# Attention and mixture of experts on one core: softmax sums as a reduction over two columns, and batches 0 and 1 in another order

## The chip, the cores and the metric

The kernel runs on one core of a Trainium2 chip. The metric is the device time of one execution in microseconds (us), the median of several runs. The engines are called as in the profile: PE (matrix multiply, with PEld for its weight loads), DVE (vector), ACT (activation), POOL (GpSimd) and SP (which issues most DMAs). Each engine takes its instructions strictly in the order of the program.

## The reference

```python
def _attn_ref(q, k, v):                    # each (8, 8, 576, 64)
    k_p = k.reshape(B, H, Sp, pool, D).mean(axis=3)   # pool = 8, Sp = 72
    v_p = v.reshape(B, H, Sp, pool, D).mean(axis=3)
    scores = scale * np.matmul(q, k_p.transpose(0, 1, 3, 2))
    scores = scores - np.max(scores, axis=-1, keepdims=True)
    attn = np.exp(scores)
    attn = attn / (np.sum(attn, axis=-1, keepdims=True) + 1e-09)
    return np.matmul(attn, v_p)
...
def _moe_ref(x, w_group, w_expert, w1, w2):   # x (4608, 512)
    # group = argmax of x @ w_group, expert = argmax of x @ w_expert[group]: top 1 of 4, then top 1 of 4
    # out[token] = g_w * e_w * (relu(x @ w1[g, e]) @ w2[g, e]); w1 (.., 512, 1024), w2 (.., 1024, 512)
```

The rows of x are the tokens, with the 8 heads of a token side by side.

## The kernel before

The work goes batch by batch (8 batches of 576 tokens). All matrix products of x are made in two parts: a value rounded to the fast format (`hi`) and the rest (`lo`), with three products for each pair. Nearly all tokens of a batch go to one expert, so the kernel guesses that expert (batches 0 and 1) or counts it (`main_expert`, later batches), loads its weights with an address from a register, and runs all 576 tokens through it. Tokens of other experts are run in a loop at the end.

For one batch, in pieces whose names stand in the plans below (`a`, `n`, `x` are the attention of the plan's batch, the next and the one after; `m`, `w` the experts' part of the plan's batch and the next):

- `load_k`, `load_v`, `load_q`/`load_qb`: DMAs from SP. `kr`, `vr`, `vm` sum k (DVE) and v (POOL) over eight rows: the folds of L257 and L258. `kt` turns k on PE. `qb` (L303, DVE) or `qt` (PE) turns q.
- for each of five chunks `c`: `sc` (scores, PE, L317), `mx` (maximum, DVE, L328), `sb` (subtract on DVE, L333, then exp on ACT, L335), `su_` (sums and reciprocals, DVE, L341 to L343), `nm` (multiply by the reciprocal, on POOL as `:p` or DVE as `:v`, L348), `pt` (transpose, DVE, L355).
- `av` (attention times v, PE, L368, then the copies of x to `xa`/`xb` on ACT, L373), `avd` (the low part of x, DVE, L377), `rt` (router products, PE), `route_g` and `route_e` (the choice of group and expert on DVE, some 17 tiny instructions, L390 to L427), `count` (PE), `gates` (L481 to L495) and `keep_x`.
- `guess_x`, `guess_e`: the guess, from the mean of v. It ends in `elect`, whose integer (L449) SP reads into a register before the weights' DMAs (`load`, L523) go out.
- `load:m:j`: a quarter of w1 (m = 1) or w2 (m = 2), four buffers in all. `cast` makes its high part (ACT, L529), `lo` its low part (POOL, L535, in 2 or 4 pieces); `split` is both.
- `up:f:half` (12 matmuls, L552), its relu (ACT, L554) and `upd` (DVE, low part of the hidden values, L560/L564); `down:z` (8 matmuls, L578/L589) and the scaled result (L583) with its store.
- `home_v` (L205 to L210) writes the sums of v of batch 0 to memory and reads them back in another layout. `warm` is matmuls on ones, with no use but to occupy PE. `split_wr` (L859, L860) makes the router's weights in two parts.

The order within each engine is written out by hand. `START` (to the first `up`), `FIRST` (rest of batch 0) and `SECOND` (batch 1) fix it for PE, SP, DVE, ACT and POOL; `STEADY` (batches 2 to 6) and `LAST` (batch 7) fix it for all but ACT, which a planner orders by its own costs. Rings of buffers: three PSUM banks `mm` for `up`, `down`, `warm` and some `sc`; one pair of banks `sc` shared by `sc` and half of `av`; three banks `tp` for the rest.

```python
LATE = 1
MANUAL = [{ET.PE, ET.SP, ET.DVE, ET.Activation, ET.Pool}, {ET.PE, ET.SP, ET.DVE, ET.Pool}]
```

Of the kernel before, what the change touches and what calls it, by code (L numbers as in the profile page):

```python
# [919 lines left out]
```

## Time and profile before

| | us |
|---|---|
| median of 3 runs (lowest, highest) | 543.24 (542.77, 543.7) |
| the profiled execution, its own time | 541.33 |
| its span, first to last instruction | 539.7 |
| busy in the span: PE, PEld | 514.7, 450.0 |
| busy in the span: DVE, POOL, ACT | 361.2, 245.4, 208.5 |
| mean granted clock of PE | 0.99 of full speed |

Positions below are us from the start of the span. The first `up` of batch 0 starts at 28.21, that of batch 1 at 104.86, that of batch 2 at 172.39, that of batch 3 at 234.3. The profiled execution's own time is 1.6 us more than its span, and 1.9 us less than the median of the runs.

### The profile page before, as it was taken

To read this page: it belongs to the slowest core of one execution; us is meant where nothing else is said; L and a number is where in the kernel's file an instruction comes from. 1 tells how busy PE (TensorE), PEld (TensorE's weight loads), DVE (VectorE), ACT (ScalarE), POOL (GpSimd) and SP (SyncE) were. 2 spreads that over 40 slices of the span, in tenths; PEclk is the share of its full clock that TensorE was granted. 3 is DMA by queue.
4 is the path that set the end of the run, shared out by engine and by line. 5 is a ranking of instruction groups with operands and counts; after the bars stand their busy time and mean duration, and the time that the engine had idled before them with its cause. 6 is when DMAs were issued, how large, how long until landed. Compare 5 with 4: busy or idle time off the path is not lost.

```text
span 539.7 us, 15043 instructions
## 1 busy us (share of the span) xinstructions
PE 514.7 (95%) x6059; PEld 450.0 (83%) x6059; DVE 361.2 (67%) x1039; ACT 208.5 (39%) x402; POOL 245.4 (45%) x217
## 2 busy tenths in 40 slices
PE   9899798979998999999999999999999999999995
PEld 7778786879876998899888998899888988899864
DVE  6787889688767886479664966578644953287602
ACT  2264323353323652354415442355325442344211
POOL 2299426155702781276508580476409661411300
PEclk9799999999999999999999999999999999999998
DMA  8599267837155594547726592779536200835711
GB/s 281 152 237 213 28 203 190 194 104 193 36 98 186 152 247 81 195 148 213 113 76 238 168 170 57 238 281 234 93 113 209 81 3 19 267 115 202 258 72 52
DMA packets 117984, 83.75 MB, mean 155 GB/s; under 512 B 71018, under 2 KB 93546, under 8 KB 117656
## 3 DMA queue, kind: packets, MB, share of 16 engines
q1 hardware_dynamic: 113904, 75.60, 52.3%
q10 hardware_dynamic: 3976, 7.12, 3.8%
q8 instruction: 49, 0.80, 0.6%
q14 instruction: 23, 0.19, 0.1%
q0 software_dynamic: 32, 0.04, 0.0%
HBM read 77.31 MB, written 28.53 MB: 196 GB/s over the span
## 4 chain that ended last, share of the span: by engine, by line
PE 76%; DVE 11%; DMA 7%; issue 2%; ACT 2%; SPq 1%; POOL 1%; ACTq 0%; DVEq 0%; POOLq 0%
PE mm L552 31%; PE mm L578 26%; PE mm L589 5%; PE sc L317 4%; DMA sw<-in_moe_w_dram 4%; PE sc L368 4%; PE tp L385 2%; DMA vv<-in_v_dram 1%; DMA out_dram<-y 1%; DVE pT L355 1%; DVE p L333 1%; DVE mx L328 1%; DVE p L348 1%; POOL w L535 1%; DVE kv L258 1%
## 5 line engine op out<-in xcount | busy, mean ns | idle before, releaser
L535 POOL TENSOR_TENSOR w<-sw,w 128x1024 fp32r<-128x1024 f32 (+2 forms) x87 | 150.0, 1741 | 154.5 <-ACT w L529 154.5
L578 PE MATMUL mm<-w,ht 128*128 128x512 f32 x768 | 177.5, 384 | 0.0
L578 PEld LDWEIGHTS mm<-w,ht 128*128 128x128 f32 x768 | 141.4, 189 | 22.1 <-issue 2.0
L552 PE MATMUL mm<-xb,w 128*128 128x320 f32 x768 | 116.4, 303 | 3.8 <-DVE es L422 1.7
L552 PEld LDWEIGHTS mm<-xb,w 128*128 128x128 f32 x768 | 106.1, 189 | 8.1 <-issue 3.7
L552 PE MATMUL mm<-xa,w 128*128 128x256 f32 x768 | 98.1, 279 | 5.7 <-DVE ht L560 3.1
L552 PEld LDWEIGHTS mm<-xa,w 128*128 128x128 f32 x768 | 91.5, 191 | 10.5 <-DVE ht L560 3.3
L554 ACT ACTIVATE ht<-mm 128x256 fp32r<-128x256 f32 (+1 forms) x128 | 52.1, 408 | 91.5 <-PE mm L552 91.3
L529 ACT CAST w<-sw 128x1024 fp32r<-128x1024 f32 x64 | 66.1, 1043 | 26.4 <-DMA sw<-in_moe_w_dram 26.4
L348 POOL TENSOR_TENSOR p<-p,su 128x576 f32<-128x576 f32 (+1 forms) x34 | 36.6, 1079 | 55.1 <-DVE su L343 51.3
L564 DVE SCALAR_TENSOR_TENSOR ht<-mm,ht 128x160 fp32r<-128x160 f32 (+2 forms) x192 | 38.6, 257 | 14.8 <-ACT ht L554 14.3
L335 ACT ACTIVATE p<-p 128x576 f32<-128x576 f32 (+1 forms) x40 | 25.5, 638 | 58.7 <-DVE p L333 57.3
L583 ACT ACTIVATE y<-mm,gm 128x512 f32<-128x512 f32 x32 | 21.9, 684 | 48.7 <-PE mm L578 45.3
L328 DVE TENSOR_REDUCE mx<-sc 128x8 f32<-128x576 f32 (+1 forms) x38 | 26.1, 687 | 20.1 <-PE sc L317 20.1
L560 DVE SCALAR_TENSOR_TENSOR ht<-mm,ht 128x256 fp32r<-128x256 f32 x64 | 26.1, 408 | 17.6 <-ACT ht L554 17.2
L317 PE MATMUL sc<-kT,qT 64*32 64x72 f32 x2176 | 30.4, 229 | 2.6 <-DVE qT L303 1.3
L317 PEld LDWEIGHTS sc<-kT,qT 64*32 64x32 f32 x2176 | 23.8, 105 | 10.2 <-issue 6.7
L355 DVE STREAM_TRANSPOSE pT<-p 128x640 f32<-128x640 f32 (+1 forms) x40 | 30.4, 761 | 1.6 <-POOL p L348 1.5
L341 DVE TENSOR_REDUCE su<-p 128x8 f32<-128x576 f32 (+1 forms) x40 | 27.0, 674 | 4.0 <-ACT p L335 3.8
L589 PE MATMUL mm<-w,ht 128*128 128x512 f32 x128 | 29.6, 381 | 0.0
L368 PE MATMUL sc<-pT,v 32*64 32x256 f32 (+1 forms) x384 | 26.9, 409 | 1.4 <-DVE pT L355 1.4
L333 DVE TENSOR_TENSOR p<-sc,mx 128x576 f32<-128x576 f32 (+1 forms) x38 | 26.4, 694 | 1.4
(213 smaller groups left out, 529.3 us busy)
## 6 DMA issues: line engine op xcount, KB each, us to landing
sw<-in_moe_w_dram SPq DMA_DIRECT2D x72, 512.0 KB
xscr<-xb SPq DMA_DIRECT2D x8, 1280.0 KB
vv<-in_v_dram SPq DMA_DIRECT2D x27, 320.0 KB
xscr<-xa SPq DMA_DIRECT2D x8, 1024.0 KB
q<-in_q_dram SPq DMA_DIRECT2D x112, 72.0 KB
kv<-in_k_dram SPq DMA_DIRECT2D x14, 512.0 KB
out_dram<-y ACTq DMA_DIRECT2D x24, 256.0 KB
pT<-xscr SPq DMA_DIRECT2D x4, 1152.0 KB
```

The costliest lines, as they stand in the source:

```text
L317: nc.tensor.matmul(ps[x][32 * g:32 * g + 32, SP * t:SP * t + SP], lhsT=s.qT[c][64 * x:64 * x + 64, g, 32 * t:32 * t + 32], rhs=s.kT[64 * x ...
L333: tt(out=p.rearrange("p t (x s) -> p x t s", x=2)[:, x], in0=ps[:, :, 0:SP * w].rearrange("p x (t s) -> p x t s", s=SP), in1=bc(s.m[c][:, ...
L348: (nc.vector if eng == "v" else nc.gpsimd).tensor_tensor(out=p, in0=p, in1=bc(s.su[c][:, 0:w], SP), op=ALU.mult)
L355: nc.vector.transpose(out=s.pT[:, :, o:o + n].rearrange("p j (t i) -> p t j i", i=32), in_=probs[(s.b * NC + c) % 2][:, 0:n // 32].rearran ...
L368: nc.tensor.matmul(banks[a][64 * x:64 * x + 64, 0:n], lhsT=s.v6[32 * a:32 * a + 32, 5 if x and i == 0 else j, :], rhs=s.pT[32 * a:32 * a + ...
L529: nc.scalar.copy(out=s.w[m, j][0], in_=raw)
L535: (nc.vector if eng == "v" else nc.gpsimd).tensor_tensor(out=wl[:, i:i + n], in0=s.raw[m, j][:, i:i + n], in1=wh[:, i:i + n].bitcast(F32), ...
L552: nc.tensor.matmul(ps[:, 0:n], lhsT=l[:, kc, fs], rhs=apart(s.a.xt[o][:, r, kc]), start=(kc == 0 and i == 0), stop=(kc == 3 and i == 2))
L554: nc.scalar.activation(out=halves(ht[:, sl]), in_=joined(ps[:, 0:n]), func=AF.Relu)
L564: stt(out=ht[:, at:at + hi - lo], in0=ps[:, a, lo:hi], scalar=0.0, in1=ht[:, t + lo:t + hi].bitcast(F32), op0=ALU.max, op1=ALU.subtract)
L578: nc.tensor.matmul(ps, lhsT=s.ht[f][:, 640 * l + o:640 * l + o + 128], rhs=apart(s.w[2, f // 2][r][:, f % 2, :]), start=(i == 0), stop=(i ...
L589: nc.tensor.matmul(ps, lhsT=s.ht[f][:, 512:640], rhs=apart(s.w[2, f // 2][r][:, f % 2, :]), start=(i == 0), stop=(i == 15))
```

## The change

1. `su_`: two standing tiles `sums` hold 1e-9 in every second column. The sum over 72 goes to the first column, and a second reduction adds the pair; the instruction that added 1e-9 and multiplied by 8 (L342) is gone. The factor of one eighth is in the copies of x: `av` multiplies by 0.125 while it copies, `avd` is a three-operand instruction that does the same.
2. `route_e` and `gates` can put their last product on POOL (`:p`).
3. `START`, `FIRST` and `SECOND` are in another order. `STEADY` and `LAST` have the same order.

```diff
 START
-t.warm:10 t.turn_wr a.kr:0 a.kr:1 a.kt a.vr:0:f a.vr:1:f a.qt:0 a.qt:1 a.sc:0 a.mx:0 a.sb:0 a.sc:1:m a.guess_x a.mx:1 a.sb:1 a.home_v a.guess_e a.vm
-m.load:1:0 m.load:1:1 m.load:1:2 m.load:1:3 a.qt:2 a.su_:0 a.nm:0:p a.qt:3 a.su_:1 a.nm:1:p t.warm:5 n.load_v n.load_k a.sc:2:m a.qt:4 a.pt:0 a.pt:1 m.cast:1:0 m.lo:1:0:p:4
-a.av:0:256 a.mx:2 a.sb:2 m.cast:1:1 m.lo:1:1:p:4 a.avd:0:256 t.split_wr
+t.warm:10 t.turn_wr a.kr:0 a.kr:1 t.split_wr a.kt a.vr:0:f a.vr:1:f a.qt:0 a.qt:1 a.sc:0 a.mx:0 a.sc:1:m t.warm:2 a.guess_x a.sb:0 a.mx:1 a.home_v a.guess_e a.qt:2 a.sb:1 a.su_:0 a.nm:0:p
+m.load:1:0 m.load:1:1 m.load:1:2 m.load:1:3 a.qt:3 a.su_:1 a.nm:1:p a.vm a.sc:2:m a.qt:4 t.warm:7 n.load_v n.load_k a.pt:0 a.pt:1 m.cast:1:0 m.lo:1:0:p:4
+a.av:0:256 a.mx:2 a.sb:2 m.cast:1:1 m.lo:1:1:p:4 a.avd:0:256
 FIRST (its first two lines stand, but for m.up:0:0, now m.up:0:0:1)
-m.up:5:0 a.pt:4 n.vr:0 m.cast:2:0 m.lo:2:0:p:2 m.upd:5:0 m.up:6:0 m.upd:6:0 a.av:256:320 m.up:7:0 a.rt:0:256 m.upd:7:0 a.avd:256:320 n.kr:0
-n.vr:1 n.vm m.up:0:1:1 m.upd:0:1 n.kr:1 a.rt:256:320 m.cast:2:1 m.lo:2:1:p:2 m.up:1:1 m.upd:1:1 m.up:2:1 a.route_g m.upd:2:1 m.up:3:1 m.cast:2:2 m.lo:2:2:p:2 a.route_e m.upd:3:1 m.up:4:1 m.upd:4:1
-n.kt m.up:5:1 m.upd:5:1 a.count n.guess_x m.cast:2:3 m.lo:2:3:p:2 n.qb:0 m.up:6:1 n.guess_e w.load:1:0 w.load:1:1 m.upd:6:1 n.sc:0 n.mx:0 n.sb:0 n.qb:1 a.gates a.keep_x m.up:7:1 m.upd:7:1
-m.down:0 n.su_:0 n.nm:0:p w.load:1:2 m.down:1 w.load:1:3 n.sc:1 n.mx:1 n.sb:1 n.pt:0 n.qb:2 m.down:2 m.store:0 x.load_v x.load_k m.down:3 n.su_:1 n.nm:1:p w.split:1:0:p:2 m.down:4 n.sc:2 n.mx:2 n.sb:2 n.pt:1 n.qb:3
-m.down:5 m.store:1 w.split:1:1:p:2 n.su_:2 n.nm:2:v n.av:0:256 n.avd:0:256 m.down:6 n.sc:3 n.mx:3 n.sb:3 n.pt:2 n.qb:4 m.down:7 n.su_:3 n.nm:3:v n.sc:4 n.mx:4 n.sb:4 m.down:8 m.store:2 x.vr:0
-n.rt:0:256 n.pt:3 n.su_:4 n.nm:4:v w.load:2:0 w.load:2:1 x.load_qb:0 m.down:9 n.pt:4 x.kr:0 m.down:10 n.av:256:320 n.avd:256:320 x.kr:1 x.vr:1 x.vm m.down:11 m.store:3 x.load_qb:1 x.load_qb:2 x.load_qb:3 n.rt:256:320 m.down:12 n.route_g m.down:13 m.store:4
+m.up:5:0 a.pt:4 n.vr:0 m.upd:5:0 m.up:6:0 m.upd:6:0 a.av:256:320 n.vr:1 n.vm m.up:7:0 a.rt:0:256 m.upd:7:0 a.avd:256:320 n.kr:0
+m.up:0:1:1 m.upd:0:1 n.kr:1 a.rt:256:320 n.guess_x m.cast:2:0 m.up:1:1 n.guess_e m.upd:1:1 a.route_g m.cast:2:1 m.up:2:1 m.upd:2:1 a.route_e:p m.lo:2:0:p:2 m.up:3:1 m.upd:3:1 m.lo:2:1:p:2 m.cast:2:2 a.gates m.up:4:1 m.upd:4:1
+a.count n.qb:0 m.lo:2:2:p:2 n.kt m.cast:2:3 m.up:5:1 m.upd:5:1 a.keep_x n.sc:0 n.mx:0 n.sb:0 n.qb:1 m.lo:2:3:p:2 m.up:6:1 w.load:1:0 w.load:1:1 m.upd:6:1 n.su_:0 n.nm:0:p m.up:7:1 m.upd:7:1
+m.down:0 w.load:1:2 n.sc:1 n.mx:1 n.sb:1 n.pt:0 n.qb:2 m.down:1 w.load:1:3 m.down:2 m.store:0 n.su_:1 n.nm:1:p x.load_v x.load_k w.split:1:0:p:2 m.down:3 n.sc:2 n.pt:1 n.mx:2 n.sb:2 n.qb:3 n.qb:4 m.down:4 n.su_:2 n.nm:2:p n.av:0:256 n.avd:0:256 w.split:1:1:p:2
+m.down:5 m.store:1 n.sc:3 n.mx:3 n.sb:3 n.pt:2 m.down:6 n.su_:3 n.nm:3:p m.down:7 n.sc:4 n.mx:4 n.sb:4 n.pt:3 x.load_qb:0 m.down:8 m.store:2 n.su_:4 n.nm:4:p x.vr:0 n.rt:0:256 w.load:2:0 w.load:2:1 m.down:9 n.pt:4 x.kr:0 n.av:256:320 n.avd:256:320
+m.down:10 x.kr:1 x.vr:1 x.vm x.load_qb:1 x.load_qb:2 x.load_qb:3 n.rt:256:320 m.down:11 m.store:3 n.route_g m.down:12 n.route_e:p n.gates:p m.down:13 m.store:4
 SECOND (its first line before and after; further down, before: m.down:7 n.route ... m.down:9 n.main_expert; after: m.down:5 n.route_g n.route_e:p ... m.down:7 n.main_expert)
-m.up:0:0 m.upd:0:0 m.split:1:2:p:2 m.load:2:2 a.route_e m.up:1:0 m.upd:1:0 m.split:1:3:p:2 m.load:2:3 m.up:0:1 m.upd:0:1 m.split:2:0:p:2 m.up:1:1 m.upd:1:1 m.up:2:0 a.count m.upd:2:0 a.gates a.keep_x m.up:2:1
+m.up:0:0 m.upd:0:0 n.qb:0 m.up:1:0 m.upd:1:0 m.split:1:2:p:2 m.load:2:2 a.count n.kt m.up:0:1 m.upd:0:1 a.keep_x m.split:1:3:p:2 m.load:2:3 m.up:1:1 m.upd:1:1 n.sc:0 n.mx:0 n.sb:0 n.qb:1 m.up:2:0 m.upd:2:0 n.su_:0 n.nm:0:p m.split:2:0:p:2 m.up:2:1 m.upd:2:1 n.sc:1 n.mx:1 n.sb:1 n.pt:0 n.qb:2
...
+    sums = [keep.tile([128, 4, 2, 2], F32, name=f"s{i}") for i in range(2)]
+    for t in sums:
+        nc.vector.memset(t, 1e-9)
...
-            su = su[:, 0:w]
-            red(out=su, in_=p.rearrange("p t (x s) -> p t x s", x=2), axis=AX.X, op=ALU.add)
-            ts(out=su, in0=su, scalar1=1e-9, scalar2=8.0, op0=ALU.add, op1=ALU.mult)
+            su, two = su[:, 0:w], sums[(s.b * NC + c) % 2][:, 0:w]
+            red(out=two[:, :, :, 0], in_=p.rearrange("p t (x s) -> p t x s", x=2), axis=AX.X, op=ALU.add)
+            red(out=su, in_=two, axis=AX.X, op=ALU.add)
...
-                nc.scalar.copy(out=xt[:, 0, g], in_=ps)
+                nc.scalar.mul(out=xt[:, 0, g], in_=ps, mul=0.125)
...
-                tt(out=s.xt[o][:, 1, g], in0=ps, in1=s.xt[o][:, 0, g].bitcast(F32), op=ALU.subtract)
+                stt(out=s.xt[o][:, 1, g], in0=ps, scalar=0.125, in1=s.xt[o][:, 0, g].bitcast(F32), op0=ALU.mult, op1=ALU.subtract)
...
-            tt(out=s.oh, in0=bc(goh, E), in1=eoh.unsqueeze(2).broadcast_to([128, NC, G, E]), op=ALU.mult)
+            (nc.gpsimd if eng == "p" else nc.vector).tensor_tensor(out=s.oh, in0=bc(goh, E), in1=eoh.unsqueeze(2).broadcast_to([128, NC, G, E]), op=ALU.mult)
...
-            tt(out=s.gm, in0=s.gm, in1=gate[:, b, :], op=ALU.mult)
+            (nc.gpsimd if eng == "p" else nc.vector).tensor_tensor(out=s.gm, in0=s.gm, in1=gate[:, b, :], op=ALU.mult)
```

## Rows read from the trace of the kernel before

**Rows 1.** Busy time by stretch: sum, PE, PEld, DVE, ACT, POOL, clock, DMA, GB/s
```profile
0.00:28.21 28.21, 24.35 (x375) 19.91 (x375) 19.06 (x54) 7.78 (x15) 6.69 (x26) 0.88 0.73 223
28.21:68.42 40.21, 36.28 (x457) 32.19 (x458) 32.91 (x86) 17.93 (x37) 30.98 (x34) 1.00 0.73 149
68.42:104.86 36.44, 34.13 (x455) 27.17 (x454) 31.70 (x72) 11.22 (x23) 15.22 (x14) 1.00 0.77 206
104.86:171.30 66.44, 62.91 (x789) 54.18 (x787) 50.35 (x143) 23.96 (x51) 25.16 (x23) 1.00 0.47 114
171.30:174.63 3.33, 1.65 (x10) 1.27 (x10) 1.64 (x2) 2.57 (x3) 2.22 (x2) 1.00 0.88 290
...
234.44:294.25 59.81, 59.81 (x719) 52.94 (x718) 40.03 (x115) 25.15 (x48) 30.61 (x24) 1.00 0.59 155
```

**Rows 2.** PE's longest wait in the first 210 us: total, times, longest
```profile
PE mm L552 <- DVE ht L560: 3.1, 1, 3.1
```

**Rows 3.** Timeline of START: start, busy, engine, line, what, count, idle before
```profile
16.69 2.81 SPq L210 DMA_DIRECT2D v<-vscr  x4
...
19.30 0.15 DVE L449 TENSOR_SCALAR me<-ct 128x1 int32<-128x1 f32 x1
...
20.57 2.15 SPq L523 DMA_DIRECT2D sw<-in_moe_w_dram  x4
...
21.69 3.38 PE L866 MATMUL mm<-ones 128*128 128x256 f32 x10
...
26.36 0.37 ACT L298 COPY qT<-tp 128x256 f32<-128x256 f32 x1 [3.91 <-PE tp L292]
...
26.63 1.05 ACT L529 CAST w<-sw 128x1024 fp32r<-128x1024 f32 x1
...
27.75 5.62 POOL L535 TENSOR_TENSOR w<-sw,w 128x256 fp32r<-128x256 f32 x8 [3.71 <-ACT w L529]
...
28.21 2.77 PE L552 MATMUL mm<-xa,w 128*128 128x256 f32 x12 [0.47 <-ACT xa L373]
```

**Rows 4.** Busy time of two stretches of 1 us, columns as in rows 1
```profile
17.00:18.00 1.00, 1.00 (x6) 1.00 (x5) 0.15 (x1) 0.68 (x1) 0.00 (x0) 0.50 0.19 42
...
24.00:25.00 1.00, 1.00 (x6) 0.59 (x6) 0.84 (x1) 0.00 (x0) 0.04 (x1) 1.00 0.99 342
```

**Rows 5.** Single source lines: count, ns min/median/max, first and last start
```profile
L342 DVE TENSOR_SCALAR su<-su x40: 170/172/1828, 20.3 to 435.4; 128x8 f32<-128x8 f32 x32, 128x4 f32<-128x4 f32 x8
...
L390 DVE TENSOR_REDUCE m<-el x8: 175/175/176, 60.8 to 454.8; 128x5 f32<-128x20 f32 x8
...
L486 DVE TENSOR_SCALAR se<-se x8: 171/172/173, 71.0 to 459.5; 128x5 f32<-128x5 f32 x8
...
L275 POOL TENSOR_TENSOR v<-v,share x16: 292/292/748, 21.2 to 414.2; 128x64 f32<-128x64 f32 x16
```

**Rows 6.** Timeline of FIRST, from 60 us on
```profile
63.71 0.70 DVE L303 STREAM_TRANSPOSE qT<-q 128x512 f32<-128x512 f32 x1
...
68.42 3.62 PE L578 MATMUL mm<-w,ht 128*128 128x512 f32 x16
```

**Rows 7.** Timeline of SECOND at its first stall
```profile
108.79 7.42 POOL L535 TENSOR_TENSOR w<-sw,w 128x512 fp32r<-128x512 f32 x6 [11.46 <-ACT w L529]
...
108.96 1.15 DVE L392 TENSOR_TENSOR de<-el,m 128x20 f32<-128x20 f32 x1
...
112.59 1.25 DVE L427 TENSOR_TENSOR oh<-og,oe 128x80 f32<-128x80 f32 x1
...
114.23 1.60 PE L552 MATMUL mm<-xa,w 128*128 128x256 f32 x12 [3.06 <-DVE ht L560]
```

**Rows 8.** Timeline at the end of SECOND
```profile
164.75 0.15 DVE L449 TENSOR_SCALAR me<-ct 128x1 int32<-128x1 f32 x1
...
165.77 4.11 SPq L523 DMA_DIRECT2D sw<-in_moe_w_dram  x4
...
171.29 1.04 ACT L529 CAST w<-sw 128x1024 fp32r<-128x1024 f32 x1 [3.79 <-DMA sw<-in_moe_w_dram]
```

More of the change, by code (lines that the diff above doesn't have):

```diff
@@ L39 @@
+m.load:1:0 m.load:1:1 m.load:1:2 m.load:1:3 a.qt:3 a.su_:1 a.nm:1:p a.vm a.sc:2:m a.qt:4 t.warm:7 n.load_v n.load_k a.pt:0 a.pt:1 m.cast:1:0 m.lo:1:0:p:4
+a.av:0:256 a.mx:2 a.sb:2 m.cast:1:1 m.lo:1:1:p:4 a.avd:0:256
 """
 FIRST = """
-m.up:0:0 a.su_:2 a.nm:2:p m.upd:0:0 a.sc:3 m.cast:1:2 m.load:2:0 m.up:1:0 a.mx:3 a.sb:3 m.lo:1:2:p:4 m.upd:1:0 a.pt:2 m.up:2:0 a.su_:3 a.nm:3:p m.cast:1:3 m.lo:1:3:p:4
+m.up:0:0:1 a.su_:2 a.nm:2:p m.upd:0:0 a.sc:3 m.cast:1:2 m.load:2:0 m.up:1:0 a.mx:3 a.sb:3 m.lo:1:2:p:4 m.upd:1:0 a.pt:2 m.up:2:0 a.su_:3 a.nm:3:p m.cast:1:3 m.lo:1:3:p:4
@@ L49 @@
+m.down:10 x.kr:1 x.vr:1 x.vm x.load_qb:1 x.load_qb:2 x.load_qb:3 n.rt:256:320 m.down:11 m.store:3 n.route_g m.down:12 n.route_e:p n.gates:p m.down:13 m.store:4
 """
 SECOND = """
-m.up:0:0 m.upd:0:0 m.split:1:2:p:2 m.load:2:2 a.route_e m.up:1:0 m.upd:1:0 m.split:1:3:p:2 m.load:2:3 m.up:0:1 m.upd:0:1 m.split:2:0:p:2 m.up:1:1 m.upd:1:1 m.up:2:0 a.count m.upd:2:0 a.gates a.keep_x m.up:2:1
-m.upd:2:1 n.kt n.qb:0 m.up:3:0 m.upd:3:0 m.split:2:1:p:2 x.load_v m.up:3:1 m.upd:3:1 n.sc:0 n.mx:0 n.sb:0 n.qb:1 m.up:4:0 m.upd:4:0 n.su_:0 n.nm:0:p m.up:4:1 m.upd:4:1
@@ L53 @@
-m.up:5:0 m.upd:5:0 m.split:2:2:p:2 n.sc:1 n.mx:1 n.sb:1 n.pt:0 n.qb:2 m.up:5:1 m.upd:5:1 n.su_:1 n.nm:1:p x.load_k m.up:6:0 m.upd:6:0 m.up:6:1 m.upd:6:1 n.sc:2 n.mx:2 n.sb:2 n.pt:1 n.qb:3 m.up:7:0 m.upd:7:0
-n.su_:2 n.nm:2:p m.split:2:3:p:2 m.up:7:1 m.upd:7:1 m.down:0 n.av:0:256 n.avd:0:256 m.down:1 n.sc:3 n.mx:3 n.sb:3 n.pt:2 n.qb:4 m.down:2 m.store:0 n.su_:3 n.nm:3:v x.load_qb:0 x.load_qb:1 x.load_qb:2 x.load_qb:3 m.down:3 n.rt:0:256 n.sc:4 n.mx:4 n.sb:4
-n.pt:3 m.down:4 n.su_:4 n.nm:4:v m.down:5 m.store:1 n.pt:4 x.kr:0 n.av:256:320 n.avd:256:320 x.vr:0 m.down:6 n.rt:256:320 m.down:7 n.route x.kr:1 m.down:8 m.store:2 x.vr:1 x.vm m.down:9 n.main_expert w.load:1:0 w.load:1:1 w.load:1:2 w.load:1:3 m.down:10
@@ L56 @@
-x.qb:0 n.gates n.keep_x x.kt m.down:11 m.store:3 w.split:1:0:p:2 w.load:2:0 x.sc:0 x.mx:0 x.sb:0 x.qb:1 m.down:12 w.split:1:1:p:2 w.load:2:1 x.su_:0 x.nm:0:p m.down:13 m.store:4
+m.up:0:0 m.upd:0:0 n.qb:0 m.up:1:0 m.upd:1:0 m.split:1:2:p:2 m.load:2:2 a.count n.kt m.up:0:1 m.upd:0:1 a.keep_x m.split:1:3:p:2 m.load:2:3 m.up:1:1 m.upd:1:1 n.sc:0 n.mx:0 n.sb:0 n.qb:1 m.up:2:0 m.upd:2:0 n.su_:0 n.nm:0:p m.split:2:0:p:2 m.up:2:1 m.upd:2:1 n.sc:1 n.mx:1 n.sb:1 n.pt:0 n.qb:2
+x.load_v m.up:3:0 m.upd:3:0 n.su_:1 n.nm:1:p m.split:2:1:p:2 m.up:3:1 m.upd:3:1 m.up:4:0 m.upd:4:0 n.sc:2 n.mx:2 n.sb:2 n.pt:1 n.qb:3 x.load_k m.split:2:2:p:2 m.up:4:1 m.upd:4:1 n.su_:2 n.nm:2:p m.up:5:0 m.upd:5:0 m.up:5:1 m.upd:5:1 n.sc:3 n.mx:3 n.sb:3 n.pt:2 n.qb:4
@@ new lines @@
+x.load_qb:0 x.load_qb:1 x.load_qb:2 x.load_qb:3 m.up:6:0 m.upd:6:0 n.su_:3 n.nm:3:p m.up:7:0 m.upd:7:0 n.av:0:256 n.avd:0:256 m.split:2:3:p:2 m.up:6:1 m.upd:6:1 n.sc:4 n.mx:4 n.sb:4 n.pt:3 m.up:7:1 m.upd:7:1 n.su_:4 n.nm:4:p m.down:0 n.pt:4 m.down:1 m.down:2 m.store:0 m.down:3 n.av:256:320 n.avd:256:320
+m.down:4 x.kr:0 x.vr:0 n.rt:0:256 n.rt:256:320 m.down:5 m.store:1 n.route_g n.route_e:p x.kr:1 m.down:6 x.vr:1 x.vm m.down:7 n.main_expert w.load:1:0 w.load:1:1 w.load:1:2 w.load:1:3 m.down:8 m.store:2 x.qb:0 n.gates n.keep_x x.kt m.down:9 w.split:1:0:p:2 w.load:2:0 m.down:10
@@ L57 @@
+x.sc:0 x.mx:0 x.sb:0 x.qb:1 m.down:11 m.store:3 w.split:1:1:p:2 w.load:2:1 x.su_:0 x.nm:0:p m.down:12 m.down:13 m.store:4
 """
@@ L417, in route_g, with route_e @@
             s.goh = goh
-        def route_e(s):
+        def route_e(s, eng="v"):
             goh, lg = s.goh, lgs[s.b % 2]
@@ L475, in guess_e, with gates @@
             s.elect(cr)
-        def gates(s):
+        def gates(s, eng="v"):
             b = s.b
```

## The prediction

> **What bounds the kernel now.** I read the busy time by stretch first. From batch 2 on, PE is never idle: 59.81 us busy in 59.81 for one batch [rows 1]. That is the floor of a batch, and the change leaves the order of batches 2 to 7 alone. So only what lies ahead of 174.63 can move: 28.21 us of START, 76.65 of FIRST, 66.44 of SECOND and 3.33 in which batch 2 starts with PE busy for 1.65 [rows 1]. SECOND holds what a batch holds plus one `sc` and one `kt`, some 61.3 by the profile's durations, so about 5 us of it are stalls. PE's waits name the longest of all stalls: 3.1 us for DVE's L560 [rows 2]. The timelines then say what DVE was doing there.
>
> **The main thing the rows show is a collision of DVE with POOL.** POOL makes low parts without a break from 108.79, six pieces in 7.42 us, 1.24 us each. In that time the router's tiny subtraction takes 1.15 us and the product `oh` 1.25 us, and PE waits 3.06 us [rows 7]. The tensor_scalar L342 has a median of 172 ns and a maximum of 1828; the tiny tensor_reduce L390 has 175 to 176 in all eight batches [rows 5]. So tensor_tensor, scalar_tensor_tensor and tensor_scalar on SBUF wait for the end of POOL's piece, and reductions don't.
>
> **The softmax sums.** L342 goes (172 ns), a reduction of 16 to 8 numbers comes; by the nearest row it costs 175 ns [rows 5]. Bounds: 0.17, and the 0.3 of a reduction with strided operands. So nothing is saved on a quiet chip, and up to 1.6 us at each collision. The multiplying copies and the three-operand `avd` read PSUM as their forerunners did; I take them at the same length, with 0.05 us each way as bounds, hidden in batches 2 to 7 by DVE at 40.03 of 59.81 and ACT at 25.15 [rows 1].
>
> **START.** The guess's integer is ready at 19.45. SP is busy with L210 until 19.50 and issues the first weights at 20.57 [rows 3]. In the new order the copy of `gx` no longer queues behind an exp, so the integer is ready at about 17.5; but SP's queue still holds `home_v` until 19.5. The weights therefore leave at 20.35 to 20.57: the earlier guess earns 0 to 0.2 us. They land near 24.2. What is earned lies behind that: the first cast began at 26.63 because the copy ahead of it on ACT (26.36) waited 3.91 us for PE, which was in `warm` from 21.69 for 3.38 us [rows 3]. Now `qt:4` stands ahead of `warm`, and the cast starts at 24.2. `up:0:0` starts 1.58 us after its cast as before (28.21 - 26.63), at 25.8: **-2.4 us**. `warm:2` fills the gap in which PE's clock fell (0.50 at 17 to 18, full again at 24 [rows 4]), so the seven later `warm` fit before `av`, near 23.
>
> **The first half of FIRST.** Its first two lines stand. POOL works without a break on 16 pieces of 0.70 us and two `nm`, from 27.75 until 41.1, and `up:6:0` waits for the last piece. It starts 2.5 us earlier; one gap of 0.55 opens, as the second cast on ACT is now later than POOL. `split_wr` no longer stands in DVE's way. I put `av:256:320` at 39.7, 2.3 us earlier.
>
> **Routing and gates of batch 0: where I expect the gain to be lost.** From 39.7 the queues give: `rt:256` 45.8, `guess_x` 46.9, `up:1:1` 47.6, `guess_e` 49.3, the router's transposes done at 50.5. POOL is through with `vr`/`vm` near 46, so nothing collides: on DVE `guess_e` takes 1.3, `upd` 0.6, `route_g` 1.75 (nine instructions, some 0.2 each), `upd` 0.6 and `route_e` 1.65, until 56.05. POOL does `oh`: 0.29 by the nearest row [rows 5], 0.24 as on DVE at the least. Then all the low parts of w2 follow, eight pieces from 56.45. Behind `upd:3:1` DVE comes to `gates` at 56.65, and its tensor_scalar, scalar_tensor_tensor and three products now meet POOL. Each ends at a piece's end (57.7, 59.0, 60.2, 61.5, 62.7): `gates` lasts 6 us instead of 1.9 (some eleven instructions like L486, 0.17 each [rows 5]). Queued behind it on DVE are `upd:4:1`, the count and `qb:0` (0.70 [rows 6]), until 64.35; `sc:0` on PE waits for `qb:0` and holds two more `up`. PE has nothing from 59.8 to 64.4. `down:0` starts at 68.5, and started at 68.42 [rows 6]: the 2.3 us are gone. Cost of `gates` from both sides: 1.9 if nothing collides, 7.5 if each waits a piece and the next.
>
> The Trainium skill, GPSIMD Engine Reference, Specifications, says that GpSimd shares its SBUF interfaces with VectorE and is in contention with instructions of two SBUF inputs or in a two-port mode. No row shows the instructions of `gates` themselves under POOL's work; by that rule they collide, and without it this part would give about 4 us.
>
> **The rest of FIRST** (36.44 us, PE busy 34.13 [rows 1]). Three `nm` go from DVE to POOL, `sc` and `av` stand further behind what they need. PE is idle for 2.3 us by the row, and for 3.3 by the gaps between the starts of its matmuls, ahead of `av`, `sc:3`, `sc:4` and the second `av`. That goes, but for half a microsecond: **-2.8 us**. POOL has 15.22 of 36.44 busy [rows 1] and takes 7 us of late low parts with it.
>
> **SECOND.** `route_e` and `gates` of batch 1 are done before POOL gets the next low parts (these need a cast behind the first relu). The 3.06 us stall goes, with two of 0.35. Against it: the attention of batch 2 moves to the front. There DVE has 5.2 us of work in the 3.8 us of two `up` and a `sc`; later stretches give it back. Walking it I find 0.2 us lost at `av` and 0.75 at `sc:4`. 66.4 becomes 62.5: **-3.9 us**.
>
> **The start of batch 2.** The integer is ready at 164.90, weights leave at 165.77, the cast starts at 171.29 [rows 8]: 5.5 us, and PE waits. Now `main_expert` stands two `down` earlier with routing further ahead still; the weights leave 10 us before SECOND's end, more than 5.5. The 3.4 us by which batch 2 exceeds the floor shrink to some 0.8: **-2.6 us**. Moved past on SP: one store and the loads of q, which are not waited for there.
>
> **Sum.** To `down:0` +0.1, then -2.8, -3.9, -2.6: -9.2. The profiled execution would take 541.33 - 9.2 = 532.1; the median stands 1.9 above it, so 543.24 - 9.2 = **534.0 us**.
>
> **Rivals.** *No collision at the gates.* If ACT is late with a cast, or POOL with `oh`, POOL pauses and `gates` takes 1.9. Then `sc:0` comes 4 to 5 us earlier: 534.0 - 4.5 = 529.5. For it: L486 in `gates` takes 171 to 173 ns in all eight batches [rows 5]. Against it: the casts are done 8 us before.
>
> *The clock falls in the new gap.* PE idle for 4.6 us before `sc:0` may bring the low clock, as around 15 us, where it stayed some 6.8 us (17 to 24 [rows 4]); half of that is lost: 534.0 + 3.4 = 537.4. Against it: around 112 us PE stood for 3.06 us [rows 7] at full clock. The Trainium skill, TensorE: Matmul & The Clock Gate, Why this matters for your kernels, warns of idle gaps between bursts; the 3.06 us row shows no loss, a longer one no row shows.
>
> *SECOND's dense front doesn't give it back.* If DVE falls behind for good by its 1.4 us at each of four chunks, SECOND keeps its old length and batch 2 part of its wait: 534.0 + 4.5 = 538.5. For it: DVE's order is strict, and `sc` has one pair of banks. Against: DVE is busy only 50.35 of 66.44 [rows 1].
>
> *Slower.* ACT's order in batches 2 to 7 is the planner's, and the planner sees new instructions. If it put one cast (1.04 us [rows 8]) ahead of a relu twice in a batch where PE has no slack, six batches would cost 12.5 us: 534.0 + 12.5 = 546.5. It decides from 1.6 us a batch on. Against it: PE stood for nothing there, and two banks of `mm` cover a late relu of 1.3 us. *Nothing happens* (543) would need START's and SECOND's gains to be eaten together.
>
> **Chances.** Forecast 0.45, no collision 0.20, the clock 0.12, SECOND 0.13, slower 0.06, nothing 0.04. The likeliest gives 534.0. To leave out no more than 2 in 10 the range goes from 529.0 (no collision) to 539.5 (SECOND with 1 us more): 529.0 to 539.5. A measurement of this kernel can tell about 0.2% (1.1 us) from no change: faster 0.90, same 0.04, slower 0.06.
>
> **What would show it.** Right: the first `up` near 25.8 with its cast near 24.2 and SP's first weights still at 20.4; `gates` stretched to about 6 us with L486 to L495 near 1.2 us each, and PE idle before `sc:0`; L342's successor never above 0.3; no stall of 3 us in SECOND; batch 2's cast before SECOND's end, and 59.8 us for each later batch. Wrong: a low clock between 60 and 70 us, `sc` in SECOND waiting for DVE time after time, weights of START landing later than 24.2, or batches 2 to 7 above 59.9.

## The result, and the profile after

The changed kernel takes 535.49 us (median of 20 runs, 533.44 to 543.35), the kernel before beside it 542.69 (20 runs): ratio 0.9862, 95% interval 0.984 to 0.9884. That is faster by 1.4%, 7.2 us; forecast were 534.0 us in a range of 529.0 to 539.5, a gain of 9.2.

The profiled execution of the changed kernel took 538.19 us (span 536.4, clock 0.987), 2.7 us over its median; that of before lay 1.4 us under the median beside it. So the positions below show only 3.1 us of the gain, and the clock has to be kept apart from the order. In this listing the code lines are shifted by two: the sums' L342 is now L344, L486 is L488, L535 is L537, L552 is L554, L578 is L580.

Busy time by stretch, as in [rows 1] (cut at the first `up` of batch 0, `down:0`, the first `up` of batch 1, the first cast and the first `up` of batch 2, and one later batch):

```profile
0.00:26.73 26.73, 24.78 (x384) 20.09 (x384) 19.29 (x57) 8.17 (x16) 9.05 (x29) 0.94 0.75 233
26.73:72.61 45.88, 38.34 (x456) 34.37 (x457) 36.61 (x100) 18.75 (x39) 27.13 (x31) 0.93 0.63 148
72.61:106.67 34.06, 34.06 (x455) 26.99 (x454) 26.77 (x63) 11.23 (x22) 18.26 (x17) 1.00 0.82 209
106.67:166.89 60.22, 59.25 (x774) 51.49 (x773) 44.25 (x130) 22.22 (x48) 28.61 (x28) 1.00 0.46 113
166.89:170.12 3.23, 3.23 (x16) 2.83 (x15) 1.35 (x4) 3.14 (x4) 2.11 (x2) 1.00 0.97 310
...
231.43:291.24 59.81, 59.81 (x719) 52.94 (x718) 38.78 (x115) 25.28 (x48) 29.68 (x20) 1.00 0.60 155
```

Against [rows 1], START is shorter by 1.5 us, the first half of FIRST is longer by 5.7, the rest of FIRST has lost all of its idle time, and a later batch is what it was, 59.81. PE's waits (line, releaser, total, times, longest; compare [rows 2]):

```profile
PE sc L319 <- DVE qT L305: 4.6, 1, 4.6
PE sc L370 <- DVE pT L357: 1.7, 1, 1.7
...
PE mm L554 <- DVE y L597: 1.0, 1, 1.0
```

The wait of 3.1 us in SECOND is gone and one of 4.6 has come, in FIRST. The timeline there:

```profile
58.09 0.33 POOL L429 TENSOR_TENSOR oh<-og,oe 128x80 f32<-128x80 f32 x1 [11.54 <-DVE oe L400]
58.37 9.85 POOL L537 TENSOR_TENSOR w<-sw,w 128x512 fp32r<-128x512 f32 x8
...
58.74 0.93 DVE L488 TENSOR_SCALAR se<-se 128x5 f32<-128x5 f32 x1
...
59.70 1.20 DVE L489 SCALAR_TENSOR_TENSOR se<-sg,se 128x5 f32<-128x5 f32 x1
...
61.04 1.16 DVE L493 TENSOR_TENSOR mp<-oh,moh 128x80 f32<-128x80 f32 x1
...
62.23 1.19 DVE L494 TENSOR_TENSOR loh<-oh,mp 128x80 fp32r<-128x80 f32 x1
...
63.60 0.96 DVE L497 TENSOR_TENSOR gm<-gm,gate 128x5 f32<-128x5 f32 x1
...
66.00 1.25 PE L319 MATMUL sc<-kT,qT 64*32 64x72 f32 x64 [4.62 <-DVE qT L305]
```

This is the collision of the forecast: POOL makes eight low parts in 9.85 us, and five instructions of `gates` that take 0.17 to 0.24 us on a quiet chip take 0.93 to 1.20. Each ends with one piece: the pieces at 59.64, 60.88, 62.10, 63.32 and 64.54, the instructions at 59.66, 60.90, 62.20, 63.42 and 64.56. DVE then does the count and `qb:0`, and PE stands for 4.62 us. What the gap does to the clock is in the stretches from 62 us on (columns as in [rows 1]):

```profile
62.00:64.00 2.00, 0.00 (x0) 0.00 (x0) 1.93 (x4) 0.00 (x0) 2.00 (x3) 1.00 0.00 0
64.00:66.00 2.00, 0.00 (x0) 0.03 (x1) 2.00 (x8) 0.00 (x0) 2.00 (x3) 0.65 0.00 0
66.00:68.00 2.00, 2.00 (x67) 1.80 (x68) 1.93 (x7) 0.00 (x0) 2.00 (x2) 0.50 0.00 0
...
70.00:72.00 2.00, 2.00 (x11) 2.00 (x11) 0.74 (x4) 0.44 (x1) 0.00 (x0) 0.64 0.76 253
```

Half clock (1.2 GHz) sets in before PE resumes and stays for some 7 us. From `sc:0` to `down:0` it is 6.61 us here (66.00 to 72.61); a trace without the gap, below, has 4.18.

The end of SECOND, to be held against [rows 8]:

```profile
160.87 0.15 DVE L451 TENSOR_SCALAR me<-ct 128x1 int32<-128x1 f32 x1
...
161.91 3.63 SPq L525 DMA_DIRECT2D sw<-in_moe_w_dram  x4
...
166.89 1.04 ACT L531 CAST w<-sw 128x1024 fp32r<-128x1024 f32 x1 [5.80 <-DMA sw<-in_moe_w_dram]
...
170.12 1.50 PE L554 MATMUL mm<-xa,w 128*128 128x256 f32 x12
...
174.55 0.68 DVE L597 TENSOR_TENSOR y<-mm,y 64x512 f32<-64x512 f32 x1 [4.80 <-ACT y L596]
...
175.29 1.60 PE L554 MATMUL mm<-xa,w 128*128 128x256 f32 x12 [1.02 <-DVE y L597]
```

PE no longer waits for the first weights of batch 2: it is busy for all of 166.89 to 170.12. But some four microseconds later it waits 1.02 us for a PSUM bank that the last `down` of batch 1 still holds.

### The profile page after: what moved, and what is told of

It reads as the page before. It is cut to its first block, busy times and chain, and to the rows that moved or that the text cites. A ratio compares the mean times of both kernels' runs of the same rounds, so it can differ in the third digit from the quotient of the medians.

```text
span 536.4 us, 15072 instructions
## 1 busy us (share of the span) xinstructions
PE 516.3 (96%) x6067; PEld 452.1 (84%) x6067; DVE 348.7 (65%) x1032; ACT 208.7 (39%) x402; POOL 250.4 (47%) x226
## 4 chain that ended last, share of the span: by engine, by line
PE 85%; DMA 5%; DVE 4%; SPq 1%; POOL 1%; issue 1%; ACT 1%; DVEq 0%; POOLq 0%; ACTq 0%
PE mm L554 34%; PE mm L580 29%; PE sc L319 5%; PE mm L591 5%; PE sc L370 4%; PE tp L387 3%; DMA vv<-in_v_dram 2%; PE mm L868 2%; DMA sw<-in_moe_w_dram 1%; DMA out_dram<-y 1%; SPq L525 1%; PE tp L282 1%; PE tp L411 1%; PE tp L370 0%; DVE p L350 0%
## 5 line engine op out<-in xcount | busy, mean ns | idle before, releaser
L537 POOL TENSOR_TENSOR w<-sw,w 128x1024 fp32r<-128x1024 f32 (+2 forms) x87 | 148.4, 1725 | 117.2 <-ACT w L531 117.0
L580 PE MATMUL mm<-w,ht 128*128 128x512 f32 x768 | 177.1, 383 | 0.0
L580 PEld LDWEIGHTS mm<-w,ht 128*128 128x128 f32 x768 | 141.5, 189 | 21.7 <-issue 2.0
L554 PE MATMUL mm<-xb,w 128*128 128x320 f32 x768 | 118.1, 306 | 0.9 <-DVE ht L562 0.9
L554 PEld LDWEIGHTS mm<-xb,w 128*128 128x128 f32 x768 | 108.0, 192 | 5.5 <-issue 2.5
L554 PE MATMUL mm<-xa,w 128*128 128x256 f32 x768 | 97.3, 278 | 2.2 <-DVE y L597 1.0
L554 PEld LDWEIGHTS mm<-xa,w 128*128 128x128 f32 x768 | 91.4, 191 | 6.3 <-DVE y L597 1.3
L556 ACT ACTIVATE ht<-mm 128x320 fp32r<-128x320 f32 (+1 forms) x128 | 51.6, 408 | 82.9 <-PE mm L554 82.8
L350 POOL TENSOR_TENSOR p<-p,su 128x576 f32<-128x576 f32 (+1 forms) x39 | 41.5, 1065 | 76.0 <-DVE su L345 63.0
L566 DVE SCALAR_TENSOR_TENSOR ht<-mm,ht 128x160 fp32r<-128x160 f32 (+2 forms) x192 | 39.0, 258 | 17.7 <-ACT ht L556 17.2
L343 DVE TENSOR_REDUCE s<-p 128x8 f32<-128x576 f32 (+1 forms) x40 | 27.1, 678 | 2.9 <-ACT p L337 2.8
```

Source lines behind the costliest of these rows:

```text
L343: red(out=two[:, :, :, 0], in_=p.rearrange("p t (x s) -> p t x s", x=2), axis=AX.X, op=ALU.add)
L350: (nc.vector if eng == "v" else nc.gpsimd).tensor_tensor(out=p, in0=p, in1=bc(s.su[c][:, 0:w], SP), op=ALU.mult)
L537: (nc.vector if eng == "v" else nc.gpsimd).tensor_tensor(out=wl[:, i:i + n], in0=s.raw[m, j][:, i:i + n], in1=wh[:, i:i + n].bitcast(F32), ...
L554: nc.tensor.matmul(ps[:, 0:n], lhsT=l[:, kc, fs], rhs=apart(s.a.xt[o][:, r, kc]), start=(kc == 0 and i == 0), stop=(kc == 3 and i == 2))
L556: nc.scalar.activation(out=halves(ht[:, sl]), in_=joined(ps[:, 0:n]), func=AF.Relu)
L566: stt(out=ht[:, at:at + hi - lo], in0=ps[:, a, lo:hi], scalar=0.0, in1=ht[:, t + lo:t + hi].bitcast(F32), op0=ALU.max, op1=ALU.subtract)
```

## The experiments

Two readings stood against each other. Mine: what the change does is move DVE's tiny instructions out of POOL's low parts in SECOND (a gain) and into them at batch 0's gates (a loss), with START and the sums worth little. The rival: the parts gain by themselves (shorter sums, earlier start, FIRST's new order), and the gap before `sc:0` is harmless or only a matter of the clock. Four kernels with one part each came first; the kernel before took 543.25 us beside them.

**The sums alone.** All of the new arithmetic, the three orders of before.

```diff
-START, FIRST, SECOND (after)
+START, FIRST, SECOND (before)
```

> The softmax sums, the eighth in the copies and the three-operand avd alone, in the old order of all batches. Theory A (the gain is in the order; the sums only spare the collisions of L342 with POOL): 0 to 1.6 us faster, ratio 0.997 to 1.000, and the successor of L342 never above 0.2 us. Theory B (the sums carry the gain, as L342 loses some 4 us of DVE in all to collisions): 4 us faster or more, ratio 0.992 or less.

Measured: 542.02 us, ratio 0.9984 (0.9949 to 1.002): no difference that can be told. The second reduction is never slowed here, but the router's subtraction is (1.13 us at 108.49), and the 3.06 us stall of PE before 113.75 is still there. So the sums and the copies are not where the gain comes from.

**START alone**, in the kernel before.

```diff
-START (before)
+START (after)
```

> The new START alone, the old arithmetic and the old FIRST and SECOND behind it. Theory A (START earns 1.5 to 2.4 us at the first up, and FIRST's chain of POOL and DVE passes on at least half of it): ratio 0.996 to 0.998, first up near 26.7. Rival (all of it is absorbed in FIRST, where POOL, DVE and the loads set the pace): ratio 0.999 to 1.001 though the first up is early.

Measured: 543.41 us, ratio 0.9984 (0.9947 to 1.0022), between the two ranges expected. In its trace the first `up` starts at 25.53, 2.7 us earlier, `down:0` 1.4 earlier and the `up` behind the router's stall 1.7 earlier. There the lead ends: `up` at 112.56 waited 3.05 us as before, but this time it runs at half clock (0.50 from 112 to 116; 1.00 in the profile of before):

```profile
112.56 2.93 PE L552 MATMUL mm<-xa,w 128*128 128x256 f32 x12 [3.05 <-DVE ht L560]
```

Twelve matmuls take 2.93 us instead of 1.60 [rows 7]. The earlier start is real; at the end of this kernel nothing of it can be measured.

**FIRST alone**, with the routing of batch 1 left in SECOND.

```diff
-FIRST (before)
+FIRST (after), without n.route_e:p n.gates:p
```

> The new FIRST alone, without the routing and gates of batch 1 at its end, with the old START, SECOND and arithmetic. Theory A (the gates collide with POOL and cost what the rest of FIRST gains): between 1.5 us faster and 2 us slower, ratio 0.997 to 1.004; PE idle some 4.5 us before the first scores of batch 1 near 66 us; the 3 us stall in SECOND stays. Rival (FIRST's order is where the gain is): 4 us faster or more, ratio 0.992 or less.

Measured: 543.88 us, ratio 1.0021 (0.9992 to 1.005). PE's 4.62 us wait is there, and the clock falls too (0.69 on the mean of 60 to 70 us):

```profile
66.21 1.25 PE L317 MATMUL sc<-kT,qT 64*32 64x72 f32 x64 [4.62 <-DVE qT L303]
```

The new order of FIRST gains nothing by itself: what its second half wins, the gates lose. In this trace the clock fell once more, in SECOND's stall: the 3.06 us wait before 115.54 is followed by half clock (0.50 from 116 to 118 us).

**SECOND alone**, with batch 1's `route_e` and `gates` at the end of FIRST.

```diff
-n.rt:256:320 m.down:12 n.route_g m.down:13                      (FIRST, before)
+n.rt:256:320 n.route_g m.down:12 n.route_e:p n.gates:p m.down:13
-SECOND (before)
+SECOND (after)
```

> The new SECOND alone, with the routing and gates of batch 1 put at the end of the old FIRST; old START, old arithmetic. Theory A (the 3 us stall of the routing and the late weights of batch 2 are the bulk of the gain): 5 to 7 us faster, ratio 0.987 to 0.991. Rival (the dense front of SECOND takes back what the stall gives): 2 us faster or less, ratio 0.996 or more.

Measured: 537.66 us, ratio 0.9909 (0.9876 to 0.9941), -4.9 us. PE's longest wait left in SECOND is 0.87 us. In this trace it is 64.21 us from the first `up` of batch 1 (104.58) to that of batch 2 (168.79), against 67.53 before, and batch 2 takes 59.92 against 61.9: 5.3 us together, with the clock at 1.00 there in both. This part carries most of the change. The four ratios make -0.9, -0.9, +1.1 and -4.9, together -5.6 us, and each is uncertain by about 2; the whole makes 7.2. Whether the parts together are worth more than their sum is therefore not shown.

The next four ran beside a kernel before of 543.54 us.

**The gates later**, where they meet only the last of the low parts.

```diff
-m.cast:2:2 a.gates m.up:4:1 ... m.upd:5:1 a.keep_x n.sc:0 ... m.up:7:1 m.upd:7:1
+m.cast:2:2 m.up:4:1 ... m.upd:5:1 n.sc:0 ... m.up:7:1 m.upd:7:1 a.gates a.keep_x
```

> The changed kernel with gates and keep_x of batch 0 moved behind the last upd of its second halves, so that qb:0 no longer queues behind the colliding gates. Theory A (that queue costs 4.8 us of idle PE, and at times the clock): PE idle under 1.5 us before the first scores of batch 1, which start near 61.5 us; clock 1.00 from 60 to 75; the first down near 67 instead of 72.6; 4 to 6 us faster than the changed kernel, ratio 0.975 to 0.979 to the kernel before. Rival (the late gates are given back at the first scaled result of down, which needs gm, or in DVE's later work): within 1.5 us of the changed kernel, ratio 0.984 to 0.988.

Measured: 532.12 us, ratio 0.9826 (0.976 to 0.9893). The gap is gone: `sc:0` runs at 60.27 and `down:0` at 64.45, and the clock is 1.00 throughout 60 to 72. Of the five instructions two still meet POOL (0.82 and 1.07 us), without holding up PE. It is 4.7 us below the changed kernel beside it (next but one), inside the 4 to 6 expected; the ratio lies between the two ranges, as that kernel itself stood at 0.989.

**The gap filled**: the collision stays, PE does `warm` in it.

```diff
-a.keep_x n.sc:0
+a.keep_x t.warm:9 n.sc:0
```

> The changed kernel with nine matmuls on ones put ahead of the first scores of batch 1, into the gap where PE stood idle. They compute nothing that is used. Theory A (the gap brings the low clock, which costs some 3 us where it falls): clock 1.00 from 62 to 74, first scores still near 66, first down near 69.5 instead of 72.6, 1.5 to 3 us faster than the changed kernel, ratio 0.980 to 0.984. Rival (the low clock in one profile was chance and costs nothing on average): ratio 0.985 to 0.989.

Measured: 534.03 us, ratio 0.985 (0.9798 to 0.9902). The gates collide as before (0.93 to 1.20 us each), PE waits 0.75 us behind 4.05 us of `warm`, and the clock stays at 1.00:

```profile
58.51 4.05 PE L868 MATMUL mm<-ones 128*128 128x256 f32 x18
...
63.31 0.88 PE L319 MATMUL sc<-kT,qT 64*32 64x72 f32 x64 [0.75 <-DVE qT L305]
```

From `sc:0` to `down:0` it is 4.17 us, against 6.61 in the changed kernel: the clock alone took 2.4 us of that execution. By the ratio alone this run would not decide between the two readings; the trace does for this one execution.

**The changed kernel again**, to stand beside these two.

> The changed kernel once more, unchanged, on the chip of these runs. Ratio 0.984 to 0.989; the first up near 26.7, gates near 6 us, PE idle some 4.8 us before the first scores; whether the clock falls there can differ from the first profile: with the low clock the span is near 536.4, without it near 533.

Measured: 536.84 us, ratio 0.989 (0.9839 to 0.994): 4.7 us over the late gates and 2.8 over the filled gap. The intervals overlap, so the order of the three rests on the medians and the traces together. The trace of this run (an execution of 543.05 us) has its first `up` at 25.57, PE's 4.62 us wait before `sc:0` at 64.99, and half clock behind it again: 6.80 us to `down:0`.

**The old FIRST** with all the rest of the change.

```diff
-FIRST (after)
+FIRST (before), with m.up:0:0:1 and n.route_g m.down:12 n.route_e:p n.gates:p m.down:13
```

> The changed kernel with the old order of FIRST (the routing and gates of batch 1 at its end, the third product of the first up kept as changed). Theory A (FIRST's new order earns in its second half what it loses at the gates): within 1.5 us of the changed kernel, ratio 0.983 to 0.989. Rival (FIRST's new order carries part of the gain): 2 us slower than the changed kernel or more, ratio 0.990 or above.

Measured: 535.78 us, ratio 0.9871 (0.9823 to 0.9918), not to be told from the changed kernel. Put in or taken out, FIRST's new order nets nothing that these runs can show (the interval is some 2.6 us to each side). Its trace has no 4.62 us wait, but one of 3.52 us for ACT's copy of `xb` before 48.18, and half clock behind that.

The last three ran beside a kernel before of 541.69 us. They ask what a step that I had missed costs (`nm:4` of batch 0, next section), whether late gates hold up a second time, and whether two more short stalls can go.

> The changed kernel with the normalisation of chunk 4 of batch 0 on POOL instead of DVE (DVE's took 2.44 us there, as it stood among POOL's low parts and value rows). Theory A (the collision costs the start's gain, but the gates' collision behind it hides whatever is earned ahead of it): av moves from 41.76 to about 41.2 and never stalls 1.9 us, and the gap ahead of sc:0 stays at 4 to 5 us; the ratio to the kernel before stays within 0.4% of the changed kernel's (0.982 to 0.990). Theory B (what is earned ahead of the gates is kept): 1 us or more below the changed kernel, ratio 0.980 to 0.984.

```diff
-a.pt:3 a.su_:4 m.upd:4:0 a.nm:4:v
+a.pt:3 a.su_:4 m.upd:4:0 a.nm:4:p
```

Measured: 535.17 us, ratio 0.9874 (0.9841 to 0.9907). `av` moves from 41.76 to 40.68, and the gap moves with it at the same length:

```profile
40.68 0.50 PE L370 MATMUL sc<-pT,v 32*64 32x320 f32 x4 [0.79 <-DVE pT L357]
...
64.92 1.25 PE L319 MATMUL sc<-kT,qT 64*32 64x72 f32 x64 [4.62 <-DVE qT L305]
```

So my reason for expecting no change was wrong: the gates don't swallow what is won ahead of them, the whole chain shifts. `down:0` came at 70.30, 2.3 us earlier than in the changed kernel, half of it because the clock was low for a shorter time (5.38 us from `sc:0`). In the time of the runs this is not to be seen.

> The version with batch 0's gates and keep_x behind upd:7:1, a second time beside the others of this call. Theory A (the collision of the gates costs about 3 us): 531 to 533 us, some 3 us below the changed kernel, no gap ahead of sc:0. Theory B (its first time was luck of the chip): 534 to 537 us, as the changed kernel.

Measured: 532.17 us, ratio 0.9823 (0.9792 to 0.9853), the first value again and 3.0 us under the run above on the same chip. PE goes through without a pause:

```profile
57.99 1.90 PE L554 MATMUL mm<-xb,w 128*128 128x320 f32 x12
59.81 0.89 PE L319 MATMUL sc<-kT,qT 64*32 64x72 f32 x64
60.63 3.53 PE L554 MATMUL mm<-xb,w 128*128 128x320 f32 x24
63.99 1.89 PE L580 MATMUL mm<-w,ht 128*128 128x512 f32 x8
```

`down:0` is 8.6 us earlier than in the profiled execution of the changed kernel (1.3 of it was won at the first `up` already, where that execution had the low clock), the first `up` of batch 1 (100.31) 6.4: a wait of 1.89 us of `av` for DVE at 77.00 gives 2 us back.

> Late gates, chunk 4's normalisation on POOL, and batch 2's product oh on DVE instead of POOL, where it took 0.97 us beside DVE's rows of batch 3 and kept PE waiting 0.87 us. Theory A (each takes a short stall away): 0.5 to 1.5 us below late gates alone, 530 to 532 us, oh of batch 2 at 0.25 us. Theory B (these stalls are covered by others, or oh on DVE queues): the same as late gates alone within 0.5 us.

```diff
-n.route_g n.route_e:p x.kr:1       (SECOND; with late gates and a.nm:4:p)
+n.route_g n.route_e x.kr:1
```

Measured: 530.75 us, ratio 0.9795 (0.9764 to 0.9827), the fastest version here, 1.4 us under late gates alone by the medians, with overlapping intervals. It has two edits more than late gates, and no run tells them apart. Batch 2's `oh` shows why it was worth a try; first with late gates alone, where POOL's `oh` runs beside DVE's sum of k, then on DVE:

```profile
150.84 0.97 POOL L429 TENSOR_TENSOR oh<-og,oe 128x80 f32<-128x80 f32 x1 [12.57 <-DVE oe L400]
...
151.87 0.45 PE L435 MATMUL tp<-oh,ones 128*128 128x80 f32 x2 [0.87 <-POOL oh L429]
```

```profile
151.47 0.24 DVE L429 TENSOR_TENSOR oh<-og,oe 128x80 f32<-128x80 f32 x1
...
151.86 0.42 PE L435 MATMUL tp<-oh,ones 128*128 128x80 f32 x2 [0.18 <-DVE oh L429]
```

## Why the prediction was right, and where its sizes were off

By the terms of its sum, in us, the profiled execution of the changed kernel against that of before. SECOND ends where the prediction cut it, at the end of batch 1's work on PE: 171.30 before, 170.12 after. Batch 3 starts at 234.3 and 231.27.

| term | forecast | measured |
|---|---|---|
| START, to the first `up` | -2.4 | -1.5 |
| from there to `down:0` (gates of batch 0) | +2.5 | +5.7 |
| rest of FIRST | -2.8 | -2.4 |
| SECOND, to the end of its last `down` | -3.9 | -3.0 |
| batch 2, from there to batch 3's first `up` | -2.6 | -1.8 |
| sum | -9.2 | -3.0 |

**The sums** were rightly costed at nothing. Their successor and the gates show both sides of the rule on which the sum rested, and they answer to L342 and L486 in [rows 5]:

```profile
L344 DVE TENSOR_REDUCE su<-s x40: 161/170/171, 19.3 to 432.4; 128x8 f32<-128x16 f32 x32, 128x4 f32<-128x8 f32 x8
L488 DVE TENSOR_SCALAR se<-se x8: 172/172/928, 58.7 to 456.5; 128x5 f32<-128x5 f32 x8
```

The reduction never exceeds 171 ns in forty calls; the tensor_scalar, never over 173 in the kernel before, takes 928 the one time that it meets POOL.

**START** was right in size, though not in this execution:

```profile
16.33 4.01 PE L298 MATMUL tp<-ident,q 128*64 128x128 f32 x32
...
17.56 0.15 DVE L451 TENSOR_SCALAR me<-ct 128x1 int32<-128x1 f32 x1
...
19.31 2.23 SPq L525 DMA_DIRECT2D sw<-in_moe_w_dram  x4
...
21.48 3.29 PE L868 MATMUL mm<-ones 128*128 128x256 f32 x14
...
22.82 1.05 ACT L531 CAST w<-sw 128x1024 fp32r<-128x1024 f32 x1 [0.80 <-DMA sw<-in_moe_w_dram]
...
26.73 2.11 PE L554 MATMUL mm<-xa,w 128*128 128x256 f32 x12 [0.48 <-ACT xa L375]
```

The integer is there at 17.7 as forecast (17.5), the cast ran even earlier than 24.2, yet `up` came at 26.73. The clock had fallen all the same, to 0.50 in 18 to 20 us; the 32 transposes took 4.01 us and `warm` ended, and `av` began, only at 24.7. Of nine traces with this START (this one and eight of the experiments) the clock fell at this place in two, and their first `up` started at 26.56 and 26.73. In a third, the first with late gates, it had fallen earlier (0.50 in 12 to 14 us, behind a wait of 1.34 us for DVE before 9.41): `warm:2` began 1.5 us later there and `up` at 26.61. The other six held full clock and have the first `up` at 25.18 to 25.68, with weights at 20.04 to 20.51 (forecast: 25.8 and 20.35 to 20.57). That `warm:2` fills the gap was too sure: it does so in six traces of nine. And in two of these six the clock fell right behind the first `up` instead: to 0.50 in 30 to 32 us in the second one with late gates, and in 28 to 34 in the fastest version, where `av:256:320` then began only at 41.87.

**The first half of FIRST** failed in this execution at one step: "I put `av:256:320` at 39.7". It began at 41.76. I had moved POOL's work but not looked at what DVE does beside it: `nm:4` took 0.54 us in the trace of before, and takes 2.44 here:

```profile
36.82 2.80 POOL L537 TENSOR_TENSOR w<-sw,w 128x256 fp32r<-128x256 f32 x4
...
38.72 2.44 DVE L350 TENSOR_TENSOR p<-p,su 128x288 f32<-128x288 f32 x1
...
39.57 1.27 POOL L259 TENSOR_TENSOR vv<-vv 128x512 f32<-128x512 f32 x1
...
41.76 0.50 PE L370 MATMUL sc<-pT,v 32*64 32x320 f32 x4 [1.71 <-DVE pT L357]
```

It waits out the low parts and the value rows behind them. With `nm:4` on POOL `av` is back at 40.68. The order alone doesn't decide this loss. Six traces have the new START, FIRST's first two lines and `nm:4` on DVE, and in all six it starts 0.1 to 0.3 us ahead of the end of one of POOL's pieces. It lost in two (this one, and 2.31 us in the changed kernel again), and took 0.45 to 0.59 us in the other four, where `av` began at 38.66 to 40.43. What decides between them stays open.

**The gates** are the step that was forecast best: five instructions stretched, six microseconds, PE idle for 4.6 from 59.8 (61.4 measured, since what lies ahead of it was late). That it is a loss of the order and can be avoided is shown by the version with late gates, measured twice at 532.1 to 532.2 us. The Trainium skill, GPSIMD Engine Reference, Specifications, says that GpSimd contends with VectorE's instructions of two SBUF inputs or in a two-port mode. This case agrees for the three products and the scalar_tensor_tensor, which read two tensors in SBUF and were stretched; the reciprocal (0.19 us) and the reduction (0.23) between them read one and were not. The tensor_scalar (0.93) reads one and was stretched; whether it ran in a two-port mode no run shows.

**The clock** was a rival of 0.12, and it belonged into the sum. I had leaned on the 3.06 us stall at full clock [rows 7]. In all four traces with the 4.62 us gap (the changed kernel twice, FIRST alone, `nm:4` on POOL) the clock fell, and from `sc:0` to `down:0` it cost 2.4 and 2.6 us in the changed kernel, 1.9 with FIRST alone and 1.2 with `nm:4` on POOL, against 3.4 in the rival's sum. The median of the runs, 535.49, lies between the 534.0 of the forecast and the 537.4 of this rival: the forecast was right in the range, but in every trace of the changed kernel it was the rival's clock that came. The Trainium skill, TensorE: Matmul & The Clock Gate, Why this matters for your kernels, warns of idle gaps between bursts of matmuls; the trace agrees for this gap, and for the shorter ones only in part (below).

**The rest of FIRST** gave 2.4, and PE was busy for all of its 34.06 us. The idle time of [rows 1], 36.44 - 34.13 = 2.3, was the right measure; my 2.8 leaned on gaps between starts of matmuls, which count time in which PE is busy.

**SECOND** gave 3.0 of 3.9 us, by the mechanism forecast:

```profile
105.84 0.18 DVE L394 TENSOR_TENSOR de<-el,m 128x20 f32<-128x20 f32 x1
...
106.73 0.33 POOL L429 TENSOR_TENSOR oh<-og,oe 128x80 f32<-128x80 f32 x1 [3.21 <-DVE sg L486]
...
106.85 0.23 DVE L488 TENSOR_SCALAR se<-se 128x5 f32<-128x5 f32 x1
```

The subtraction that took 1.15 us takes 0.18, `oh` 0.33 instead of 1.25 [rows 7]. The size was too large from the start: "about 5 us of it are stalls" came from summed durations, while [rows 1] leave PE idle for only 66.44 - 62.91 = 3.5. The losses walked at `av` and `sc:4` did not come. The one wait left is another, of 0.86 us before 157.28: the router's count for batch 2 waits for `oh`, which is now on POOL and took 0.97 us beside DVE's sum of k; before, the count waited 0.18.

**The start of batch 2** gave 1.8 of 2.6. PE's wait of 1.19 us for the first weights is gone, but "shrink to some 0.8" left out what else the batch waits for. The copy of the last `y` stands on ACT behind two casts that wait for weights, so DVE's L597 frees its PSUM bank only at 175.2, and `up` waits 1.02 us for that. Batch 2 takes 61.2 us from its first `up` to the next batch's, before 61.9; the floor is 59.81. The wait is not in every trace: with SECOND alone batch 2 takes 59.92 us, in the second one with late gates 59.81.

In the runs the gain is 7.2 us, of 9.2. The profiled execution shows 3.1; 1.3 of the rest is START's clock (26.73 against 25.40 in the second trace with late gates), and up to 2.4 the clock behind the gap. Taken at full clock in both places its sum would be -6.7, an estimate from these rows, which is near the -7.2 of the medians. How often the clock falls in unprofiled runs can't be read, and stays open. No slowing by the planner was seen in batches 3 to 6: 59.81 us each, as before.

## What to carry to other kernels

Where two engines get in each other's way, list both queues on one clock before moving either: a step that is pulled ahead must be laid against what the other engine does in its new place, down to 0.2 us instructions, and so must the steps that it pushes. A stretch of tiny dependent two-operand instructions belongs where the neighbour is idle or behind work that nobody waits for; here one such move was worth another 3 to 5 us by the medians. A gap of a few microseconds on the matmul engine costs its length and, in some executions, the slow stretch behind it, so it should be priced with both.
